# Moving the first table's product, three pairs of stores and a clearing in a kernel of windowed attention and experts

## The chip, the core and the metric

The kernel runs on one core of a Trainium2 chip. A core has five engines with an instruction queue each, and they run side by side: TensorE (PE in the profile, its weight loads PEld) multiplies matrices, VectorE (DVE) and ScalarE (ACT) do elementwise work, GpSimd (POOL) does elementwise work and the indirect transfers, and SyncE (SP) only starts transfers. Each queue is worked off in order; an instruction that waits holds up everything queued behind it on its engine. The metric is device time in microseconds, the median of several runs.

## The reference

Two blocks stand one behind the other. The first is causal attention with a window of 64 positions, over 8 sequences of 576 positions with 8 heads of 64. The second sends each of the 4608 rows of the attention's output to one of 8 experts, by the largest of 8 gate logits, and multiplies the expert's result by the softmax weight of that gate.

```python
scores = scale * np.matmul(q, k.transpose(0, 1, 3, 2))
mask = (rel >= 0) & (rel < window)
scores = np.where(mask, scores, -1000000000.0)
...
x = np.ascontiguousarray(attn_out.transpose(0, 2, 1, 3)).reshape(B * S, H * D)
...
expert_idx = np.argmax(logits, axis=1)
...
h = np.maximum(x_sorted[lo:hi] @ w1[e], 0.0)
y_sorted[lo:hi] = h @ w2[e]
...
return (gate_w[:, None] * y).astype(np.float32)
```

The gate's weight is positive and the hidden layer is a ReLU without bias, so the kernel multiplies the rows by that weight before the experts instead of after them.

## The kernel before

**Attention.** The 8 sequences are taken in four pairs, and each pair's 8 heads in four groups of two heads: 16 units. A unit has 9 blocks of 128 rows, taken three at a time, so there are 48 steps, numbered 0 to 47. `step(s)` is a pipeline written out by hand; on each engine the order of the instructions is the order in which Python emits them:

- the scores of step s+1 (`scored`, TensorE, L697), masked with a running maximum (`masked`, VectorE, L710) and put through the exponential (`softened`, ScalarE, L720). The scores use banks 0 and 1 of PSUM, the memory that TensorE writes; the next step's scores need them back from L710.
- the weighted values of step s-1 (`weighted`, TensorE, L743), into bank 6, which must have been read by the division of the step before (`divided`, VectorE, L753 to L757).
- gate logits of step s-3 (`logit`, L780); the transposes of the exponentials of step s (`flipped`, L728), each half copied out by VectorE or ScalarE (L730); the division; loads for later units; transposes of q and k for step s+3 (`turned`, L656 and L664) and of the finished rows for step s-2 (`x_turned`, L768).
- last, whatever has been put down for this step in the dictionary `todo`.

**Routing.** When the logits of a pair are complete, `after` spreads the pair's routing over the following steps through `todo`. `choose` finds the expert of each row and its rank within the expert (VectorE, L811 to L867, its second half at L847 to L867); `place` writes one-hot rows `lo` with the position within a table column (VectorE, L871, two instructions for each of nine blocks); `weigh` multiplies a block of 128 rows by its gate weight, in place (GpSimd, L882, or ScalarE, L880, for two of the third pair's nine blocks); `store` writes three blocks to `x_dram` (L891, and L898 for the last 64 rows of a sequence).

**First tables.** After the third pair, six steps on, `first_tiles` makes a table `perm_e` of the rows for the first two tiles of expert 0 from the first three pairs: VectorE forms `key` and `hi_e` (L973, L976), TensorE multiplies `lo` by `hi_e` in 54 small products (L983), VectorE turns the result into row numbers (L986). Then `gather_first` clears each of the two halves of `xg` (GpSimd, L293) and fetches rows of `x_dram` into it by indirect transfer (L295). `gather_first` is called a second time behind the loop, for the second tile. The rows are read from `x_dram`, so a fetch waits until the stores have landed.

**Experts.** Behind the loop the first tile is turned (`turn`, L316) and goes through the expert's two products (`hidden`, L354; `output`, L398), each with seven block products instead of eight; the sums of weight blocks that this needs are made by GpSimd (L142, and L1033 for the first weights). The routing of the fourth pair is woven into that tile. Then `expert(e)` runs over the 8 experts with tiles of 256 rows.

**Loads.** `load_qk`, `load_rests` and `load_v` bring q, k and v. `load_rests(bg)` loads the last 64 rows of a pair's sequences: q and k at L624, v at L628. GpSimd copies v into a shifted layout (L636, L638, L642). The queue of SyncE also brings the two halves of the first expert's second weights (L1033, at steps 42 and 45). The end of `after`, for the third pair:

```python
for n in (0, 0, 1, 2, 2):
    do(n, part)
for m in range(NTB):
    do(3 + m // 3, partial(place, bg * NTB + m))
    do((2, 2, 3, 3, 4, 4, 4, 5, 5)[m], partial(weigh, bg, m, nc.scalar if m in (2, 6) else G))
    if m % ST == ST - 1:
        do(3 + m // ST, partial(store, bg, m // ST, G))
do(6, first_tiles)
```

Of the kernel before, what the change touches and what calls it, by code (L numbers as in the profile page):

```python
# [24 lines left out]
def _ins(ap: bass.AP, axis: int, n: int) -> bass.AP:  # L25

    dims = [list(d) for d in ap.ap]
    dims.insert(axis, [0, n])
    return bass.AP(tensor=ap.tensor, offset=ap.offset, ap=dims)


def _inner(ap: bass.AP, n: int) -> bass.AP:
    return _ins(ap, len(ap.ap), n)
# [3 lines left out]
def kernel(  # L37
# [10 lines left out]
    nc = tc.nc  # L48
    P = nc.NUM_PARTITIONS
    B, H, S, D = q.shape  # L50
# [9 lines left out]
    SM = NV * P  # L60
    BG = 2
# [41 lines left out]
    V, G = nc.vector, nc.gpsimd  # L103
# [51 lines left out]
    def sums_w2(e):  # L155
        form(right_sums(G, s2s[e % NW], *w2q(e)))
# [23 lines left out]
    with tc.tile_pool(name="tmp", bufs=1) as tmp:  # L180
# [8 lines left out]
        for i in range(BG):  # L189
# [12 lines left out]
            out=before[:], in_=ones[:], pattern=[[1, P]], compare_op=ALU.is_gt, fill=0.0, base=0,  # L202
# [42 lines left out]
    ST = 3  # L245
# [12 lines left out]
    xg_all = qk_m(0, C, DM)  # L258
    xg = [xg_all[:, c] for c in range(C)]
# [29 lines left out]

    def gather_first(tokens):  # L290

        for c in range(C):
            G.memset(xg[c], 0.0)  # L293

            G.indirect_dma_start(  # L295
                out=xg[c], out_offset=None, in_=x_dram[0 : NT - BG * S, :],
                in_offset=bass.IndirectOffsetOnAxis(ap=tokens[:, c : c + 1], axis=0),
                bounds_check=NT - BG * S - 1, oob_is_err=False,
            )
# [265 lines left out]
    with tc.manual_schedule(), ExitStack() as held, ExitStack() as brief:  # L565
# [51 lines left out]
        def load_rests(bg):  # L617

            at = 6144 + bg % 2 * 2048
            vr = qk_m(at + 1024, BG, H, D)  # L620
            rests[bg] = [qk_m(at, H, D), qk_m(at + 512, H, D), vr]
            for t, src, queue in zip(rests[bg], (q, k), (nc.sync, nc.sync if bg else nc.scalar)):
                for i in range(BG):
                    queue.dma_start(  # L624
                        out=t[i * D : (i + 1) * D], in_=src[bg * BG + i, :, SM:S, :].rearrange("h p d -> p h d")
                    )
            for i in range(BG):
                nc.sync.dma_start(out=vr[D:P, i], in_=v[bg * BG + i, :, SM:S, :].rearrange("h p d -> p h d"))  # L628

        def load_v(u):  # L630
            bg, g = units[u]
# [39 lines left out]
        def blocks_of(t):  # L671

            return [(t // NV, t % NV * 2 + a) if t < BG * NV else (a, NB - 1) for a in range(2)]
# [29 lines left out]
        def masked(s, scs):  # L703

            m0 = (1, 0, 2)[s % NST]
            prs = [att.tile([P, ST, P], F32, name=f"pr{h}") for h in range(2)]
            mx = small.tile([P, 2, ST], F32, name="mx")
            for h in range(2):
                for m in range(ST):
                    V.tensor_tensor_reduce(  # L710
                        out=prs[h][:, m, :], in0=scs[h][:, m, :], in1=mask[:, m0 + m, :], scale=-scale, scalar=-2 * MASKED,
                        op0=ALU.add, op1=ALU.min, accum_out=mx[:, h, m : m + 1],
                    )
            return prs, mx

        def softened(prs, mx):
            for h in range(2):
                for m in range(ST):
                    y = prs[h][:, m, :]
                    nc.scalar.activation(out=y, in_=y, func=AF.Exp, scale=-1.0, bias=mx[:, h, m : m + 1])  # L720
            return prs
# [12 lines left out]
        def weighted(s, pTs):  # L734
            u, c = divmod(s, NST)
            bg, g = units[u]
            va, vb = v_ring[u % NVR]
            px = banks[6 if s < N - 2 else s - N + 2](0, 2, ST, VW)
            for m in range(ST):
                for a, (bp, i) in enumerate(blocks_of(c * ST + m)):  # L740
                    vt = va[:, bp, i // 2] if i % 2 or i == 0 else vb[:, bp, i // 2 - 1]
                    for h in range(2):
                        nc.tensor.matmul(  # L743
                            px[a * D : (a + 1) * D, h, m, :], lhsT=pTs[h][:, m, a * D : (a + 1) * D],
                            rhs=vt[:, h, :], start=True, stop=True, skip_group_check=True,
                        )
            return px
# [25 lines left out]
        def logit(s):  # L773

            u, c = divmod(s, NST)
            bg, g = units[u]
            if g == 0 and c == 0:
                lgs[bg] = banks[7](0, NST, P)[0 : ST * GE]
            for m in range(ST):
                nc.tensor.matmul(  # L780
                    lgs[bg][m * GE : (m + 1) * GE, c, :], lhsT=wg[:, g, :], rhs=xTs[s][:, m * P : (m + 1) * P],
                    start=(g == 0 and c == 0), stop=(g == NG - 1), skip_group_check=True,
                )
            return g == NG - 1
# [113 lines left out]
                    engine.dma_start(out=x_dram[t0 + SM : t0 + S, :], in_=x[i * D : (i + 1) * D, ST - 1, :])  # L898

        gates = {}  # L900
        todo = {}


        def slot_table(hi):
# [42 lines left out]
        def after(s, routing, bg):  # L947

            do = lambda n, op: todo.setdefault(s + n, []).append(op)
            part = lambda: next(routing, None)  # L950
            if bg < last - 1:
                for n in range(5):
                    do(n, part)

                for m in range(NTB):
                    do(5 + m * 2 // 3, partial(place, bg * NTB + m))
                    do(5 + m * 2 // 3, partial(weigh, bg, m, G))
                    if m % ST == ST - 1:
                        do(5 + m * 2 // 3, partial(store, bg, m // ST, G))
                return  # L960
# [4 lines that stand above are left out]
                do(3 + m // 3, partial(place, bg * NTB + m))  # L965
                do((2, 2, 3, 3, 4, 4, 4, 5, 5)[m], partial(weigh, bg, m, nc.scalar if m in (2, 6) else G))
                if m % ST == ST - 1:
                    do(3 + m // ST, partial(store, bg, m // ST, G))
            do(6, first_tiles)

        def first_tiles():

            V.scalar_tensor_tensor(  # L973
                out=key[:], in0=rkhi[:, 0:NJE], scalar=1.0, in1=oh_all[:, 0, 0:NJE], op0=ALU.add, op1=ALU.mult
            )
            V.tensor_tensor(  # L976
                out=hi_e[:], in0=_inner(key[:], NE * C), in1=_ins(hi_id[:, C + 1 : C + 1 + NE * C], 1, NJE),
                op=ALU.is_equal,
            )
            slots = banks[next(tr_ring)](0, NE * C)  # L980
            for j in range(NJE):
                for i in range(2):
                    nc.tensor.matmul(  # L983
                        slots, lhsT=lo[:, i, j], rhs=hi_e[:, j], start=(i + j == 0), stop=(i + j == NJE)
                    )
            V.tensor_scalar(out=perm_e[:], in0=slots, scalar1=-1.0, scalar2=float(NT), op0=ALU.mult, op1=ALU.add)  # L986
            gather_first(perm_e[:, 0:C])

        N = NU * NST
        load_qk(0)  # L990
# [19 lines left out]
        def step(s):  # L1010
            if 0 <= s + 1 < N:
                prs[s + 1] = softened(*masked(s + 1, scored(s + 1)))
            if 0 <= s - 1 < N:
                px = weighted(s - 1, pTs.pop(s - 1))
            ripe = 0 <= s - 3 < N and logit(s - 3)
            if 0 <= s < N:
                pTs[s] = flipped(prs.pop(s))
            if 0 <= s - 1 < N:
                divided(s - 1, px)
            if s >= 0 and s % NST == 0:  # L1020
                u = s // NST
                if u + 3 < NU and (u + 3) % NG == 0:
                    load_rests((u + 3) // NG)
                if u + 2 < NU:
                    load_v(u + 2)
                if u + 3 < NU:
                    load_qk(u + 3)
            if s + 3 < N:
                turned(s + 3)
            if 0 <= s - 2 < N:  # L1030
                x_turned(s - 2)
            for op in todo.pop(s, ()):
                op()  # L1033
            if ripe:
                bg, c = (s - 3) // (NG * NST), (s - 3) % NST
                parts = by_tokens(bg, c)
                next(parts)
                todo.setdefault(s + 1, []).append(partial(next, parts, None))
                if c == NST - 1:
                    after(s + 1, choose(bg), bg)  # L1040
# [4 lines left out]
            todo.setdefault(s, []).append(partial(nc.sync.dma_start, out=w2s[0][:, fs], in_=w2v[0][:, fs]))  # L1045
        for s in range(-3, N):
            step(s)
        assert not todo
        sums_w2(0)


# [45 lines left out]
        table = slot_table(hi)  # L1097
# [134 lines left out]
```

## Time and profile before

| | us |
|---|---|
| median of 3 runs (lowest, highest) | 706.89 (705.32, 711.82) |
| the profiled execution, its own time | 708.33 |
| its span in the profile | 706.5 |
| mean granted clock of TensorE, share of full | 0.989 |
| GpSimd, weighing L882: 25 instructions, each | 1.56 |
| GpSimd, clearing L293: 4 instructions, each | 0.54 |
| GpSimd, fetch of the first tables L295: 4 instructions, each | 1.05 |
| GpSimd, stores L891 and L898: 12 and 6 issues, each | 0.73 and 0.58 |

The profile is one execution, taken by the hardware profiler. In the page a line of a group has the source line, the engine, the operation, output and inputs by their names in the program, the count and the time. A line of the timeline has the start, the time from there to the end of the last merged instruction, the engine, and in brackets how long the engine had been idle and what ended it. A bracket with "issue" means that nothing which the profile shows ended the wait. A wait for several semaphores is put down to the one that came last by the profile; where the engine named had long been done, it was another, often a transfer. The line numbers are those of the kernel before.

### The profile page before, as it was taken

To read this page: it belongs to the slowest core of one execution; us is meant where nothing else is said; L and a number is where in the kernel's file an instruction comes from. 1 tells how busy PE (TensorE), PEld (TensorE's weight loads), DVE (VectorE), ACT (ScalarE), POOL (GpSimd) and SP (SyncE) were. 2 spreads that over 40 slices of the span, in tenths; PEclk is the share of its full clock that TensorE was granted. 3 is DMA by queue.
4 is the path that set the end of the run, shared out by engine and by line. 5 is a ranking of instruction groups with operands and counts; after the bars stand their busy time and mean duration, and the time that the engine had idled before them with its cause. 6 is when DMAs were issued, how large, how long until landed. Compare 5 with 4: busy or idle time off the path is not lost. (4 is left out here: it accounts for less than half of the span.)

```text
span 706.5 us, 18016 instructions
## 1 busy us (share of the span) xinstructions
PE 678.2 (96%) x6894; PEld 594.9 (84%) x6894; DVE 502.8 (71%) x1657; ACT 262.4 (37%) x665; POOL 356.4 (50%) x368
## 2 busy tenths in 40 slices
PE   5999999999889999999999999699999999999996
PEld 4888888888769898897999899599779799789995
DVE  3677998898956868766776586466777676766764
ACT  4888888788745011211111121011121121122211
POOL 4414649487573107856462356437345757254022
PEclk9999999999989999999999999899999999999999
DMA  9987889987433361531701161152127171111022
GB/s 194 221 218 178 185 179 240 217 208 194 164 108 120 107 238 62 216 132 55 266 31 61 59 246 55 64 208 92 62 61 253 61 250 65 63 39 47 16 62 61
DMA packets 137160, 94.64 MB, mean 134 GB/s; under 512 B 116591, under 2 KB 116607, under 8 KB 137024
## 3 DMA queue, kind: packets, MB, share of 16 engines
q1 hardware_dynamic: 114752, 36.19, 21.0%
q0 software_dynamic: 9120, 28.60, 12.4%
q10 hardware_dynamic: 13152, 28.05, 11.2%
q8 instruction: 83, 1.36, 0.8%
q14 instruction: 53, 0.43, 0.2%
HBM read 73.94 MB, written 20.45 MB: 134 GB/s over the span
## 5 line engine op out<-in xcount | busy, mean ns | idle before, releaser
L325 DVE STREAM_TRANSPOSE v_m<-qk_m 32x256 f32<-32x256 f32 x320 | 139.3, 435 | 7.0 <-DMA qk_m<-x_dram,at_g 1.0
L285 POOL DMA_INDIRECT qk_m<-x_dram,at_g x42 | 45.0, 1072 | 169.2 <-DVE v_m L325 160.4
L354 PE MATMUL bank<-qk_m,s 128*128 128x128 f32 x1024 | 123.2, 276 | 0.0
L354 PEld LDWEIGHTS bank<-qk_m,s 128*128 128x128 f32 x1024 | 119.1, 193 | 0.5 <-issue 0.5
L354 PE MATMUL bank<-qk_m,w 128*128 128x128 f32 x768 | 95.8, 278 | 6.2 <-issue 6.2
L720 ACT ACTIVATE pr<-pr,mx 128x128 f32<-128x128 f32 x288 | 89.7, 390 | 31.8 <-DVE mx L710 31.5
L354 PEld LDWEIGHTS bank<-qk_m,w 128*128 128x128 f32 x768 | 91.8, 194 | 9.4 <-issue 9.0
L710 DVE CUSTOM_DVE_ANT_0 pr<-bank,mask 128x128 f32<-128x128 f32 x288 | 64.4, 285 | 24.8 <-PE bank L697 23.6
L305 POOL DMA_INDIRECT out_dram<-v_m,at_s x42 | 42.6, 1013 | 56.6 <-DVE v_m L394 50.5
L394 DVE TENSOR_TENSOR v_m<-bank,v_m 128x256 f32<-128x256 f32 (+1 forms) x95 | 43.7, 479 | 37.8 <-PE bank L398 27.3
L638 POOL COPY v_m<-v_m 64x520 f32<-64x520 f32 x32 | 19.8, 617 | 67.1 <-DMA v_m<-in_v_dram 58.6
L142 POOL TENSOR_TENSOR s<-w 128x1024 f32<-128x1024 f32 x22 | 52.2, 2373 | 0.0
L743 PEld LDWEIGHTS bank<-v_m,pT 128*64 128x64 f32 x1152 | 40.6, 139 | 10.2 <-issue 4.3
L361 ACT COPY qk_m<-bank 128x512 f32<-128x512 f32 x16 | 9.4, 586 | 106.4 <-PE bank L354 80.5
L743 PE MATMUL bank<-v_m,pT 128*64 128x65 f32 x1152 | 47.4, 229 | 1.2 <-DVE xs L757 1.1
L398 PE MATMUL bank<-qkT_m,v_m 128*128 128x256 f32 x216 | 48.3, 379 | 0.0
L697 PE MATMUL bank<-qkT_m 64*64 64x128 f32 x1152 | 45.6, 287 | 0.4 <-DVE mx L710 0.3
L364 DVE TENSOR_TENSOR qk_m<-bank,qk_m 128x512 f32<-128x512 f32 x16 | 11.1, 691 | 48.6 <-PE bank L354 48.6
L398 PEld LDWEIGHTS bank<-qkT_m,v_m 128*128 128x128 f32 x216 | 41.0, 190 | 5.5
L337 ACT COPY qk_m<-v_m 128x512 f32<-128x512 f32 x40 | 22.7, 615 | 61.4 <-DVE v_m L325 61.4
L728 PE MATMUL bank<-ident,pr 128*128 128x128 f32 x288 | 43.3, 288 | 0.0
L664 PE MATMUL bank<-ident,qk_m 128*128 128x128 f32 x256 | 35.8, 286 | 6.8 <-DMA qk_m<-in_q_dram 6.8
(196 smaller groups left out, 1264.4 us busy)
## 6 DMA issues: line engine op xcount, KB each, us to landing
w<-in_moe_w_dram ACTq DMA_DIRECT2D x9, 2048.0 KB, 8.1
qk_m<-in_q_dram SPq DMA_DIRECT2D x72, 128.0 KB, 3.6
qk_m<-in_k_dram SPq DMA_DIRECT2D x66, 128.0 KB, 3.4
v_m<-in_v_dram SPq DMA_DIRECT2D x64, 128.0 KB, 3.2
qk_m<-in_moe_w_dram ACTq DMA_DIRECT2D x3, 2048.0 KB, 10.2
w<-in_moe_w_dram SPq DMA_DIRECT2D x2, 2048.0 KB, 14.2
x_dram<-xs POOLq DMA_DIRECT2D x6, 512.0 KB, 4.8
x_dram<-xs POOLq DMA_DIRECT2D x3, 768.0 KB, 6.2
```

What stands on the lines that cost most here:

```text
L142: op()
L285: G.indirect_dma_start(out=xg[c], out_offset=None, in_=x_dram[:, :], in_offset=bass.IndirectOffsetOnAxis(ap=at_g[:, c : c + 1], axis=0),)
L305: put = G.indirect_dma_start(out=out[:, :], out_offset=bass.IndirectOffsetOnAxis(ap=at_s[:, c : c + 1], axis=0), in_=ys[c], in_offset=None ...
L325: V.transpose(out=xn[b * QD : (b + 1) * QD, :, :, a * QD : (a + 1) * QD].rearrange("p c g i -> p (c g) i"), in_=rows[a * QD : (a + 1) * QD ...
L354: nc.tensor.matmul(acc[:, f, :], lhsT=a[:, g, f * P : (f + 1) * P], rhs=b[:, g, :], start=(first and f == 0 and g == 0), stop=(g == HG - 1 ...
L394: plus = lambda out, a, b: V.tensor_tensor(out=out, in0=a, in1=b, op=ALU.add)
L398: nc.tensor.matmul(acc, lhsT=a[:, f, :], rhs=b[:, f, :], start=(start and f == 0), stop=(stop and f == HF - 1), skip_group_check=True,)
L697: nc.tensor.matmul(out_, lhsT=qT[rows, t, a * WINDOW : (a + 1) * WINDOW], rhs=rhs, start=True, stop=True, skip_group_check=True,)
L710: V.tensor_tensor_reduce(out=prs[h][:, m, :], in0=scs[h][:, m, :], in1=mask[:, m0 + m, :], scale=-scale, scalar=-2 * MASKED, op0=ALU.add, ...
L720: nc.scalar.activation(out=y, in_=y, func=AF.Exp, scale=-1.0, bias=mx[:, h, m : m + 1])
L728: nc.tensor.transpose(out=tr[:, m, :], in_=prs[h][:, m, :], identity=ident[:])
L743: nc.tensor.matmul(px[a * D : (a + 1) * D, h, m, :], lhsT=pTs[h][:, m, a * D : (a + 1) * D], rhs=vt[:, h, :], start=True, stop=True, skip_ ...
```

## The change

Four edits:

- `first_tiles` becomes a generator in two parts. The first part, `key` and `hi_e`, stays where it was, in `todo` six steps on (step 45). The second part, the 54 products, `perm_e` and the fetch, goes into a new dictionary `between`, for the step after that (step 46), where `step` runs it behind the scores and the weighted values and ahead of the gate logits.
- The stores of the third pair go from GpSimd's queue to SyncE's.
- `gather_first` clears both halves of `xg` with one instruction ahead of both fetches.
- The v rows of the first pair's last 64 positions are loaded from GpSimd's queue instead of SyncE's.

On TensorE the 54 products move behind 24 score products and 24 value products; on VectorE the instruction that makes `perm_e` moves behind six of the mask (L710); on SyncE six stores stand between the two halves of the weights of L1033. No product, copy or byte is added or removed.

```diff
     def gather_first(tokens):
 
+        G.memset(xg_all, 0.0)
         for c in range(C):
-            G.memset(xg[c], 0.0)
-
             G.indirect_dma_start(
...
             for i in range(BG):
-                nc.sync.dma_start(out=vr[D:P, i], in_=v[bg * BG + i, :, SM:S, :].rearrange("h p d -> p h d"))
+                (nc.sync if bg else G).dma_start(out=vr[D:P, i], in_=v[bg * BG + i, :, SM:S, :].rearrange("h p d -> p h d"))
...
-        todo = {}
+        todo, between = {}, {}
...
                 if m % ST == ST - 1:
-                    do(3 + m // ST, partial(store, bg, m // ST, G))
-            do(6, first_tiles)
+                    do(3 + m // ST, partial(store, bg, m // ST, nc.sync))
+            table = first_tiles()
+            do(6, partial(next, table))
+            between.setdefault(s + 7, []).append(partial(next, table))
...
                 op=ALU.is_equal,
             )
+            yield
             slots = banks[next(tr_ring)](0, NE * C)
...
             V.tensor_scalar(out=perm_e[:], in0=slots, scalar1=-1.0, scalar2=float(NT), op0=ALU.mult, op1=ALU.add)
             gather_first(perm_e[:, 0:C])
+            yield
...
             if 0 <= s - 1 < N:
                 px = weighted(s - 1, pTs.pop(s - 1))
+            for op in between.pop(s, ()):
+                op()
             ripe = 0 <= s - 3 < N and logit(s - 3)
...
-        assert not todo
+        assert not todo and not between
```

## The prediction

> **What bounds the kernel now.** I read the busy shares first, then whom TensorE waited for, then stretches around the place that the change touches, and last the instructions there in order of time. Times in parentheses are starts in us of the one profiled execution. The shares, from the page:
>
> ```profile
> PE 678.2 (96%) x6894; PEld 594.9 (84%) x6894; DVE 502.8 (71%) x1657; ACT 262.4 (37%) x665; POOL 356.4 (50%) x368
> ```
>
> TensorE is busy for 678.2 of 706.5 us, so only 28.3 us of idling can be won at all, plus time at a low clock. The list of waits shows 6.8 us of it on the first q loads and 2.7 us on `hi_e` (L976), the operand of the first table's product. The stretches around that wait:
>
> ```profile
> 174.00:184.00 10.00, 8.34 (x143) 6.68 (x141) 8.55 (x50) 7.01 (x22) 3.90 (x4) 1.00 0.30 108
> 184.00:196.00 12.00, 11.41 (x202) 9.16 (x201) 11.85 (x54) 9.38 (x26) 8.95 (x8) 1.00 0.62 218
> 196.00:199.00 3.00, 0.29 (x11) 0.25 (x10) 2.60 (x19) 2.60 (x8) 2.70 (x4) 1.00 0.22 53
> 199.00:206.00 7.00, 7.00 (x114) 5.82 (x110) 2.65 (x17) 2.34 (x7) 3.45 (x5) 0.51 0.42 133
> 206.00:210.00 4.00, 4.00 (x68) 3.33 (x68) 1.92 (x7) 1.34 (x3) 3.89 (x3) 1.00 0.24 70
> ```
>
> Columns: stretch, length, busy time (and count) of TensorE, its weight loads, VectorE, ScalarE, GpSimd, then the granted clock. VectorE is full from 184 to 196 and TensorE is not; TensorE stands still from 196 to 199; then it runs at a clock of 0.51 for seven microseconds. In order of time:
>
> ```profile
> 195.55 0.49 PE L768 MATMUL bank<-ident,xs 128*128 128x128 f32 x3
> 196.86 0.55 DVE L730 COPY pT<-bank 128x384 f32<-128x384 f32 x1
> 198.43 0.27 DVE L976 TENSOR_TENSOR hi_e<-key,hi_id 128x108 bf16<-128x108 bf16 x1
> 198.75 1.56 PE L983 MATMUL bank<-hi_e,lo 128*128 128x4 bf16 x54 [2.71 <-DVE hi_e L976]
> 200.24 1.56 PE L697 MATMUL bank<-qkT_m 64*64 64x128 f32 x24
> 201.73 1.62 PE L743 MATMUL bank<-v_m,pT 128*64 128x65 f32 x24
> 203.04 1.13 POOL L295 DMA_INDIRECT qk_m<-x_dram,perm_e  x1 [3.28 <-DVE mx L710]
> 203.85 1.54 PE L728 MATMUL bank<-ident,pr 128*128 128x128 f32 x6
> 205.97 0.97 PE L743 MATMUL bank<-v_m,pT 128*64 128x65 f32 x24
> ```
>
> The product L983 is queued ahead of scores (L697) and weighted values (L743) that do not need it. The gather's wait is put down to VectorE's L710, but `perm_e` was done at 200.58; what ended it were the stores into `x_dram`, the last issued at 198.66 (their row: 2.3 to 4.8 us to landing). After 206, TensorE's largest waits carry no releaser but "issue" (6.2 us, at branches) and the rest sum to 3 us: what it gains before L316 (209.56) reaches the end one for one.
>
> **What the Trainium skill says here.** (1) TensorE: Matmul & The Clock Gate, "What's actually happening": the clock halves after an idle window of about 3.4 us, free-running, and comes back after a busy one. The trace agrees: 2.71 us of idling was followed by 0.51; 1.42 us at 182.3 was not. (2) SBUF — State Buffer, "Who interferes with whom": VectorE and GpSimd share a port pair as a lock; copies, casts, tensor_scalar and two-SBUF-input operations can be blocked. It agrees: six `lo` instructions (L871) take 1.33 us (184.49 to 185.82) with GpSimd idle, 2.40 (188.45 to 190.84) and 2.14 (193.46 to 195.60) beside its weighing. The lock is not held throughout, though: L814 took its usual 0.28 beside a weighing (123.55). (3) DMA: Bandwidth & Descriptors, "Two DMAs through the same engine are not ordered": a read of what a DMA wrote must wait for its completion, as the gather does. (4) Same page, "Latency and other measured facts": first byte about 0.6 us from SyncE's path, 1 us from GpSimd's.
>
> **The change, part by part.**
>
> *The product behind scores and values.* At stake: idling from 196.04 (195.55+0.49) to 198.75, 2.71 us, and the cold stretch. From 198.75 to 205.97, 7.22 us, TensorE does L983, L697, L743, L780, L728, L768. Warm, start to start, the same groups took 0.82, 0.90, 0.35, 0.71 and 0.42 (188.28 to 191.70); L983 took 1.49 cold, halved 0.75 (an estimate). Sum 3.95, so coldness costs 3.27. In the new order the scores wait for their bank, which L710 frees at 196.94: start 197.1, idle 1.06, end 197.9. The values wait for L757 (198.30) and ScalarE's copy of `pT` (198.45): start 198.6, idle 0.6 to 0.7. `hi_e` is ready at 198.70, so L983 runs at 199.5 without waiting. Then L780, L728, L768 to 201.7. VectorE does L710 from 198.7 to 200.0, `perm_e` to 200.5, L730 to 201.6, L753 to L757 to 202.5; the next values start at 202.65, idle about 0.85. Before: 205.97. **Gain 3.3 us**: 5.98 at stake less about 2.6 of new waits. If the clock fell nevertheless, 3.3 come back.
>
> *`perm_e` on VectorE* (0.16 us) now stands behind six L710; its only reader is the gather. Cost 0.
>
> *Stores of the third pair on SyncE.* GpSimd loses six issues, 0.82+1.32+0.60+0.75+0.56 = 4.05 us, and this:
>
> ```profile
> 186.97 0.82 POOL L891 DMA_DIRECT2D x_dram<-xs  x1 [8.07 <-issue]
> ```
>
> It stood 8.07 us for ScalarE's share of the weighing (L880, 185.70 to 186.43) with five weighings queued behind. Freed, its seven (1.56 each) run from 175.79 to 186.7, not to 197.0. SyncE issues in order behind L880's second part (189.77 to 190.52): six stores at 0.33 to 0.58, last by about 193; with 4.8 us they land by 198, not 203. Behind them on SyncE stands only `w2`'s second half: from 188.06 to about 193.5, landing at most 6.5 later, by 200; its reader, the second L142, comes at about 205. Cost 0. The gather then waits for `perm_e`: 200.7 instead of 203.04.
>
> *One clearing.* Two memsets of 0.54 become one of about 1.07, done in GpSimd's idle time. The second gather follows at 1.3 us (as at 244.08 and 245.39) instead of 1.94: 202.0, landing 3.4 later at 205.4. L316 comes at 209.56-3.3 = 206.2: not waiting, 0.8 in hand. GpSimd's L142 (9.4 us) and second gathers shift too; they keep about 3.5 us ahead of L316 at 225.68. Value 0, but without these edits the gather's old landing, 208.4, would eat 2.2 of the 3.3.
>
> *First v rests by GpSimd.* SyncE's queue moves up 1.36 us (6.75 to 8.11). TensorE's only waits for loads are ahead of that, so 0. GpSimd issues two transfers behind L992 (9.36); the trace has no such row, nearest is L991, 0.98, so to 11.3, landing (3.7 to 4.3) by 15.6. L636 moves from 11.38 to there, but the next copy waits for v until 17.62 anyway. Bounds: -0.3 (less crowding ahead of the 0.60 us wait) to +1.0 (copies later than L743 at 19.17, slack 0.37). I take 0.
>
> *The shared port, not in the diff.* Weighing moves from 187.8-197.0 to 178.9-186.7. Relief for L871: 1.07+0.81 = 1.9. In return the routing chain L847 to L867 (179.18 to 181.95, 2.77 us, GpSimd idle then) is stretched: by L871's ratio 2.27/1.33, +2.0. VectorE runs without a gap from there to `hi_e`, so these nearly cancel; I take 0. Bounds: -1.9 (no stretch) to +2.9 (blocked until 186.7, +4.8, less 1.9).
>
> **Sum:** -3.3. The profiled execution: 706.5 span, 708.33 in all, to 705.0. It lay 1.44 above the median of 706.89 (705.32 to 711.82); against the median, **703.6**. A measurement here tells about 1% (7 us) from no change, so this lies within.
>
> **Rivals.**
> 1. *The cold stretch moves forward.* The stretched chain delays L710 and L730; TensorE's gap at 182.3 grows from 1.42 to 3.4 us, the size of a window. Then about 3.3 us are lost there: -3.3+3.3, **706.9**. For it: VectorE is the bound there. Against: the stretch is only inferred. Chance 0.27.
> 2. *Slower: the port lock at the routing chain.* Each of its ten or so instructions loses to a weighing, up to the end of weighing at 186.7: +4.8-1.9, and the gap surely cools the clock, +3.3: -3.3+2.9+3.3 = +2.9, **709.8**. It decides from a stretch of 2.0 us with a cold clock, 5.2 without. For it: L820 took 1.16 instead of 0.23 beside a GpSimd sum (79.95). Against: L814. Chance 0.14.
> 3. *The idling stays where it was*, another operand (bank, `pT`) taking `hi_e`'s place and cooling the clock again: only 2.71-2.6, **706.8**. Chance 0.10.
> 4. *The gain is larger*, over 7 us, which only a second stall that I do not see could give: about 699. Chance 0.04.
>
> **Numbers.** My forecast 0.45, own range 701.2 to 705.5 (no stretch at all: -5.2; some new waits longer: -1.4). The range 700.8 to 708.4 takes in cases 1 and 3 with the 1.0 of the v rests, and leaves out 2 and 4. Over 1% faster 0.10 (case 4 and a low draw), within 0.82, slower 0.08 (a larger form of case 2).
>
> **What would show it.** Right: L983 behind L743 with no wait on `hi_e`; clock 1.00 from 196 on; GpSimd's weighings in one block ending near 187; the gather waiting for `perm_e` only, L316 not waiting for it. Wrong: L847 to L867 longer than 2.8 us, a gap over 2.5 us before L768 near 183, a clock below 0.9 anywhere between 180 and 206, or L743 later than 19.2 at the start.

## The result, and the profile after

The changed kernel takes 705.33 us (median of 20 runs, 703.58 to 708.72), the kernel before 708.15 us (705.32 to 712.52) in as many. The ratio is 0.9956, 95% interval 0.9942 to 0.9969: **faster by 0.44%**, 3.1 us by the ratio. The profiled execution spans 703.6 us, against 706.5 before. In the changed kernel the line numbers stand a little differently: scores L696, mask L709, values L742, `pT` L729, `x_turned` L767, routing L846 to L866, `lo` L870, weighing L881, product L985, fetch L294, turn L315, hidden layer L353.

First the stretches that were shown of before (start and end, length, busy time and count of TensorE, its weight loads, VectorE, ScalarE, GpSimd, then the granted clock):

```profile
174.00:184.00 10.00, 7.71 (x138) 6.18 (x136) 8.64 (x46) 5.58 (x18) 9.34 (x8) 1.00 0.29 107
184.00:196.00 12.00, 11.49 (x194) 9.38 (x194) 10.73 (x55) 10.60 (x30) 3.25 (x3) 0.86 0.63 219
196.00:199.00 3.00, 2.52 (x44) 2.09 (x43) 2.90 (x20) 2.60 (x8) 0.00 (x0) 1.00 0.81 270
199.00:206.00 7.00, 7.00 (x145) 5.78 (x143) 4.14 (x22) 3.58 (x10) 3.38 (x3) 1.00 0.22 54
```

The stand from 196 to 199 us (0.29 busy before, 2.52 now) is gone, and so is the clock of 0.51 behind it. But a clock of 0.86 has appeared from 184 to 196. TensorE's timeline of the changed kernel shows both ends of this:

```profile
178.97 0.97 PE L742 MATMUL bank<-v_m,pT 128*64 128x65 f32 x24
...
184.51 0.62 PE L767 MATMUL bank<-ident,xs 128*128 128x128 f32 x3 [2.55 <-DVE pT L729]
185.06 1.56 PE L696 MATMUL bank<-qkT_m 64*64 64x128 f32 x24
186.54 1.62 PE L742 MATMUL bank<-v_m,pT 128*64 128x65 f32 x24
...
198.69 1.02 PE L742 MATMUL bank<-v_m,pT 128*64 128x65 f32 x24 [0.48 <-DVE xs L756]
199.65 1.51 PE L985 MATMUL bank<-hi_e,lo 128*128 128x4 bf16 x54
...
202.64 1.22 PE L742 MATMUL bank<-v_m,pT 128*64 128x65 f32 x24
...
206.47 1.46 PE L315 MATMUL bank<-ident,qk_m 128*128 128x128 f32 x8
```

The product stands behind the values and waits for nothing. The same place near 184 us in the kernel before:

```profile
183.74 0.55 PE L768 MATMUL bank<-ident,xs 128*128 128x128 f32 x3 [1.42 <-DVE pT L730]
184.21 0.89 PE L697 MATMUL bank<-qkT_m 64*64 64x128 f32 x24
185.03 0.97 PE L743 MATMUL bank<-v_m,pT 128*64 128x65 f32 x24
```

The gap ahead of L767 is 2.55 us, where it was 1.42, and the scores and values behind it take the cold 1.56 and 1.62 us instead of 0.89 and 0.97. What made the gap longer is VectorE's routing chain (L846 to L866), beside GpSimd's weighing. Two timelines of the changed kernel, and between them the first and the last instruction of the chain in the kernel before, where no weighing stands beside them:

```profile
178.82 0.55 DVE L846 TENSOR_TENSOR_SCAN r_inc<-keep,r_ranks 128x72 f32<-128x72 f32 x1
...
180.21 0.63 DVE L856 TENSOR_TENSOR r_rank<-r_rank,r_ranks 128x72 f32<-128x72 f32 x1
...
181.69 0.62 DVE L864 CAST rkhi<-r_half 128x9 f32<-128x9 int32 x1
...
182.56 0.64 DVE L866 CAST low<-r_half 128x9 f32<-128x9 int32 x1
```

```profile
179.18 0.30 DVE L847 TENSOR_TENSOR_SCAN r_inc<-keep,r_ranks 128x72 f32<-128x72 f32 x1
...
181.78 0.17 DVE L867 CAST low<-r_half 128x9 f32<-128x9 int32 x1
```

```profile
175.43 10.82 POOL L881 TENSOR_SCALAR xs<-xs,gate 128x512 f32<-128x512 f32 x7 [0.62 <-DVE gate L841]
...
202.29 1.16 POOL L294 DMA_INDIRECT qk_m<-x_dram,perm_e  x1 [15.04 <-DVE perm_e L988]
203.76 1.02 POOL L294 DMA_INDIRECT qk_m<-x_dram,perm_e  x1 [0.31 <-issue]
```

Four instructions that take 0.17 to 0.30 us without company take 0.55 to 0.64, about one for each weighing that passes (10.82/7 = 1.55 us). From its start to the first mask behind it the chain takes 3.8 us instead of 2.7. The weighing is one block, and what releases the fetch is `perm_e`.

### The profile page after: what moved, and what is told of

Its sections match the earlier page's. It is cut to its first block, busy times and chain, and to the rows that moved or that the text cites. A ratio compares the mean times of both kernels' runs of the same rounds, so it can differ in the third digit from the quotient of the medians.

```text
span 703.6 us, 18017 instructions
## 1 busy us (share of the span) xinstructions
PE 674.5 (96%) x6894; PEld 591.9 (84%) x6894; DVE 502.6 (71%) x1657; ACT 262.5 (37%) x665; POOL 354.7 (50%) x362
## 5 line engine op out<-in xcount | busy, mean ns | idle before, releaser
L353 PE MATMUL bank<-qk_m,s 128*128 128x128 f32 x1024 | 122.4, 275 | 0.0
L353 PEld LDWEIGHTS bank<-qk_m,s 128*128 128x128 f32 x1024 | 118.3, 192 | 0.0
L353 PE MATMUL bank<-qk_m,w 128*128 128x128 f32 x768 | 95.8, 278 | 6.6 <-issue 6.6
L353 PEld LDWEIGHTS bank<-qk_m,w 128*128 128x128 f32 x768 | 92.0, 194 | 10.1 <-issue 9.7
L709 DVE CUSTOM_DVE_ANT_0 pr<-bank,mask 128x128 f32<-128x128 f32 x288 | 64.5, 288 | 20.3 <-PE bank L696 18.0
L742 PEld LDWEIGHTS bank<-v_m,pT 128*64 128x64 f32 x1152 | 41.3, 139 | 11.9 <-issue 4.2
L742 PE MATMUL bank<-v_m,pT 128*64 128x65 f32 x1152 | 48.5, 229 | 2.5 <-DVE xs L756 1.1
L696 PE MATMUL bank<-qkT_m 64*64 64x128 f32 x1152 | 44.3, 282 | 0.8 <-DVE mx L709 0.8
```

Source lines behind the costliest of these rows:

```text
L353: nc.tensor.matmul(acc[:, f, :], lhsT=a[:, g, f * P : (f + 1) * P], rhs=b[:, g, :], start=(first and f == 0 and g == 0), stop=(g == HG - 1 ...
L696: nc.tensor.matmul(out_, lhsT=qT[rows, t, a * WINDOW : (a + 1) * WINDOW], rhs=rhs, start=True, stop=True, skip_group_check=True,)
L709: V.tensor_tensor_reduce(out=prs[h][:, m, :], in0=scs[h][:, m, :], in1=mask[:, m0 + m, :], scale=-scale, scalar=-2 * MASKED, op0=ALU.add, ...
L742: nc.tensor.matmul(px[a * D : (a + 1) * D, h, m, :], lhsT=pTs[h][:, m, a * D : (a + 1) * D], rhs=vt[:, h, :], start=True, stop=True, skip_ ...
```

## The experiments

The table puts all of them side by side; the ratio is to the kernel before in runs on the same chip. "Start" is when the values of step 42 begin, the last ones ahead of the gap near 184 us; "section" runs from there to the first hidden-layer product; "gap" is TensorE's idle time ahead of L767 near 184, "clock" the mean granted one from 184 to 196 us; "tail" runs from the end of the last store's issue to the end of the span. All but the ratios come from one profiled execution each.

| kernel | ratio (95%) | start | section | gap | clock | tail |
|---|---|---|---|---|---|---|
| before | | 179.3 | 32.0 | 1.42 | 1.00 | 4.2 |
| before_again | 1.0010 (0.9985 to 1.0034) | 181.6 | 32.0 | 1.41 | 1.00 | 4.3 |
| product_only | 1.0047 (1.0032 to 1.0062) | 182.5 | 31.2 | 1.42 | 1.00 | 4.4 |
| stores_only | 1.0074 (1.0041 to 1.0107) | 178.8 | 31.8 | 2.55 | 0.86 | 9.3 |
| stores_only_spare | 0.9988 (0.9962 to 1.0014) | 182.9 | 30.5 | 2.54 | 0.86 | 4.9 |
| v_only | 0.9971 (0.9954 to 0.9989) | 177.7 | 31.2 | 1.42 | 1.00 | 4.4 |
| product_v | 0.9998 (0.9976 to 1.0020) | 179.5 | 31.6 | 1.42 | 1.00 | 4.4 |
| v_by_sync | 1.0056 (1.0036 to 1.0077) | 180.2 | 31.0 | 2.55 | 0.72 | 9.3 |
| v_by_sync_spare | 0.9987 (0.9968 to 1.0007) | 181.5 | 30.4 | 2.54 | 0.86 | 4.5 |
| the changed kernel | 0.9956 (0.9942 to 0.9969) | 179.0 | 29.6 | 2.55 | 0.86 | 4.5 |
| two_clearings | 0.9952 (0.9935 to 0.9970) | 179.8 | 30.5 | 2.54 | 0.86 | 4.7 |
| gate_late | 0.9949 (0.9932 to 0.9966) | 177.6 | 30.2 | 2.01 | 0.90 | 4.3 |
| weigh_scalar | 0.9923 (0.9895 to 0.9951) | 179.7 | 28.2 | 1.66 | 1.00 | 4.9 |
| no_gpsimd_weighing | 0.9896 (0.9863 to 0.9928) | 177.6 | 27.1 | 1.42 | 1.00 | 4.3 |

**One edit alone, one edit undone.** Product_only is the kernel before with nothing but the generator and `between`; stores_only has nothing but the stores' new queue; two_clearings is the changed kernel with the old clearing:

```diff
-                    do(3 + m // ST, partial(store, bg, m // ST, G))
+                    do(3 + m // ST, partial(store, bg, m // ST, nc.sync))
```

```diff
-        G.memset(xg_all, 0.0)
         for c in range(C):
+            G.memset(xg[c], 0.0)
```

> The kernel before with one edit: the 54 products stand behind the next scores and values. Theory A (the product's place is the source of the gain, and the fetch then limits it): no wait for hi_e, clock near 1.00 after 196 us, but GpSimd still ends its weighing near 197 and the stores land near 203, so the fetches start near 203 and 205 as before and L316 waits for the second until about 208; ratio to before 0.997 to 0.999. Rival B (the stores are the source): ratio 1.000. If the fetch does not limit: 0.994.

> The kernel before with one edit: SyncE stores the third pair. Theory A: GpSimd's weighing runs in one block to about 187, VectorE's routing chain is stretched by about 1.1 us beside it and TensorE goes cold for one window there; TensorE still waits for hi_e near 199, but less (about 1.9 instead of 2.7 us, since it comes later), so whether it goes cold a second time is open: ratio 0.997 without, 1.001 with it. Rival B: 0.996, all of the gain.

> The changed kernel with a clearing ahead of each fetch again. Theory A: the second fetch follows the first at 1.9 instead of 1.45 us, and L316 waits about 0.5 us longer for it: ratio to before 0.9960 to 0.9967. Rival (the fetch is hidden): 0.9956.

And the changed kernel with the first v rests back on SyncE:

```diff
-                (nc.sync if bg else G).dma_start(out=vr[D:P, i], in_=v[bg * BG + i, :, SM:S, :].rearrange("h p d -> p h d"))
+                nc.sync.dma_start(out=vr[D:P, i], in_=v[bg * BG + i, :, SM:S, :].rearrange("h p d -> p h d"))
```

> The changed kernel with the first v rests back on SyncE. Theory A: TensorE's only wait for loads at the start is for what is loaded ahead of them; the lead of 1.3 us at 22 us was down to 0.4 by 34 us; ratio to before 0.9956 to 0.9965. Rival C (a third or more of the gain is the earlier start): 0.997 or more.

For only one of the four did a forecast hold as it was meant: the rival's for two_clearings (0.9952, no difference). Each large edit alone made the kernel slower, and undoing the small one cost 1%, more than the whole change had brought. For stores_only and v_by_sync the table says where: not in the attention part, but in a tail of 9.3 us.

**The tail.** In v_by_sync the last store is issued at 701.49 + 1.00, as early as in the kernel before (702.3), and the span ends at 711.8. The lines of the program's end show GpSimd's last drains (operation, count; shortest, median and longest in ns; first and last start), first v_by_sync, then the changed kernel:

```profile
L1232 POOLq DRAIN  x3: 46/109/9148, 701.8 to 711.5; - x3
```

```profile
L1232 POOLq DRAIN  x3: 46/109/4245, 698.4 to 703.4; - x3
```

No engine works in those nine microseconds, and the longest drain is 4.9 us longer. Another trace shows itself a few instructions earlier. Among the late transfers of GpSimd in the kernel before, one waits 1.90 us for nothing that the profile names; in the changed kernel another one waits 1.53:

```profile
678.13 1.02 POOL L305 DMA_INDIRECT out_dram<-v_m,at_s  x1 [1.90 <-issue]
```

```profile
694.48 0.99 POOL L285 DMA_INDIRECT qk_m<-x_dram,at_g  x1 [1.53 <-issue]
```

The kernel before issues 108 transfers from GpSimd, and the pause lies ahead of the fifth from the end; the changed kernel issues 104 (six stores less, two loads more), and it lies ahead of the third from the end. Stores_only and v_by_sync issue 102; there all late transfers follow with the usual 0.3 to 0.4 us, and the long drain comes instead. So the theory was that the pause comes after a certain amount of GpSimd's transfers, hidden where it falls ahead of a transfer and seen where it falls on the end of the program. If so, two more transfers of any kind must take it out of the tail:

```diff
                 nc.sync.dma_start(out=vr[D:P, i], in_=v[bg * BG + i, :, SM:S, :].rearrange("h p d -> p h d"))
+                if bg == 0:
+                    G.dma_start(out=vr[0:D, i], in_=v[bg * BG + i, :, SM:S, :].rearrange("h p d -> p h d"))
```

> The changed kernel with the first rows of v again by SyncE, and two further loads of the same rows by GpSimd at the place in its queue where the v loads stood; they go into a part of the buffer that nobody reads. So only who brings the v rests differs from the changed kernel, and the number of GpSimd's transfers is the changed kernel's (104, not 102). Tail theory: v_by_sync lost about 5 us after its last store was issued (GpSimd's last drain 9.1 us instead of 4.2, span end 9.3 us after that issue ended instead of 4.5), because of how many transfers GpSimd's queue had handled. Then this one has a last drain of 4 to 5 us and a ratio near 1.0056 - 0.0069 = 0.999, down to 0.9955 if the start costs nothing. Start theory: v by SyncE is what costs, through copies and first values; then the ratio stays at 1.0056 within 0.002 and the drain says nothing of it.

> The kernel before with the third pair's stores on SyncE alone, and the same two further loads on GpSimd (104 transfers instead of 102). Tail theory: last drain of 4 to 5 us instead of 9.1; ratio 1.0074 - 0.0069 = 1.0005, within 0.998 to 1.002, which is what the stores alone are worth while the product still stands ahead of the scores. Theory that the stores hurt in the attention part: ratio stays at 1.005 or more and the drain at 9.

With 104 transfers both tails are short again (4.5 and 4.9 us), the pause is back ahead of the last gather (1.53 us in both), and the ratios fell by 0.0069 and 0.0086: **5 to 6 us hung on two transfers that nobody reads**. That what GpSimd has issued decides the tail is shown. What is counted is open: the pause stands behind 103 transfers in the kernel before and behind 101 in the changed kernel, so it isn't their number alone, and with 110 transfers (v_only and product_v) no such pause shows at all. The Trainium skill (DMA: Bandwidth & Descriptors, "SWDGE vs HWDGE vs iDMA") says that GpSimd itself writes the descriptors of its transfers into rings, and that only one queue of this kind is allocated. No run here shows the rings or what the pause is.

So stores_only and v_by_sync say nothing of the attention part by their times, and the spare versions take their place. **The stores alone are worth 0.9988**, not distinguishable from nothing.

**The first v rests.** The changed kernel and v_by_sync_spare differ only in who brings the v rests (v_by_sync_spare's two idle loads stand in their place on GpSimd, and both have the pause of 1.53 us at the same transfer), and the ratios are 0.9956 and 0.9987: 2.2 us, where the prediction had 0. To see it without any other edit, and the spread of doing nothing beside it:

```diff
-                nc.sync.dma_start(out=vr[D:P, i], in_=v[bg * BG + i, :, SM:S, :].rearrange("h p d -> p h d"))
+                (nc.sync if bg else G).dma_start(out=vr[D:P, i], in_=v[bg * BG + i, :, SM:S, :].rearrange("h p d -> p h d"))
```

> The kernel before with the first v rests loaded by GpSimd and nothing else changed (110 transfers of GpSimd, last drain about 4 us, so that the tail is that of the kernel before). Start theory, from the changed kernel against v_by_sync_spare (0.9956 against 0.9987): SyncE's queue runs 1.4 us earlier and the first values no longer wait for v (1.7 to 1.9 us in the executions of product_only and v_by_sync_spare, none or 0.7 with GpSimd): 1.5 to 3 us faster, ratio 0.996 to 0.998; step 42 by 179.0. The prediction's step: worth 0, ratio 0.9985 to 1.0015.

> The kernel before, once more, as a measure of what no change at all gives. Product_only has the same instructions on every engine up to 190 us, and yet its profiled execution reached the values of step 42 at 182.5 us where the one of the kernel before had 179.3. Theory that the start differs from execution to execution: ratio within 0.9985 to 1.0015, and the values of step 42 anywhere from 178 to 183 us. Theory that the start of a kernel is fixed and product_only's is slow for a reason of its own: 179.3 within 0.3 us.

V_only has 0.9971, 2.1 us: the same again, and outside the interval of the unchanged kernel run once more (the two intervals just overlap). Before_again has the same instructions as the kernel before, and yet its profiled execution reaches step 42 at 181.6 us instead of 179.3. The seven executions with v on SyncE lie between 178.8 and 182.9 us (mean 181.0), the seven with v on GpSimd between 177.6 and 179.8 (mean 178.7). TensorE's waits in the first 60 us (what waited, for what, total, times, longest), before_again and then v_only:

```profile
PE bank L664 <- DMA qk_m<-in_q_dram: 4.7, 1, 4.7
PE bank L743 <- ACT pr L720: 1.5, 1, 1.5
PE bank L743 <- DVE mx L710: 1.2, 1, 1.2
PE bank L743 <- POOL v_m L642: 0.8, 1, 0.8
```

```profile
PE bank L664 <- DMA qk_m<-in_q_dram: 6.2, 2, 5.8
PE bank L743 <- POOL v_m L642: 0.7, 1, 0.7
```

In before_again the first weighted values (L743) wait 2.7 us more. In product_only and v_by_sync_spare 1.9 and 1.7 us of it is put down to the loads of v themselves. Those are queued on SyncE behind the v rests: they start at 13.75 us in the kernel before and at 11.83 in v_only. GpSimd's first copy of v, which waits for them, moves up with them (the kernel before, then v_only):

```profile
17.62 0.62 POOL L638 COPY v_m<-v_m 64x520 f32<-64x520 f32 x1 [5.95 <-DMA v_m<-in_v_dram]
```

```profile
16.38 0.62 POOL L638 COPY v_m<-v_m 64x520 f32<-64x520 f32 x1 [2.74 <-DMA v_m<-in_v_dram]
```

The waits alone would mislead, since the first q come at another time in each execution. The end of the first weighted values is a better mark: 20.14 us in the kernel before, 20.27 in before_again, 18.35 in v_only; over the seven executions with v on SyncE 18.8 to 20.9 (mean 19.9), over the seven with v on GpSimd 17.9 to 18.8 (mean 18.4). So about 1.6 of the 2.3 us between the two means at step 42 are there from the first values on.

**The product without the stores.** Product_only had a late start (182.5 us) by the same kind of waits. With the v rests on GpSimd the product's own effect can be read:

```diff
+                (nc.sync if bg else G).dma_start(out=vr[D:P, i], in_=v[bg * BG + i, :, SM:S, :].rearrange("h p d -> p h d"))
...
+            for op in between.pop(s, ()):
+                op()
```

> The kernel before with the product behind scores and values and the first v rests by GpSimd; the third pair's stores stay on GpSimd, ahead of the fetch. If product_only's 1.0047 came from its start, this one starts like the changed kernel and has the product's gain of 2 to 3 us less the wait of L316 for the late fetch (1.2 us in product_only): ratio 0.996 to 0.999. If the product's place costs time by itself: 1.0015 or more.

0.9998 fits neither. Against v_only (0.9971) the product's move cost 1.9 us instead of bringing 2 to 3, though the two intervals overlap at their ends. The timeline of product_v shows why:

```profile
205.19 1.21 PE L743 MATMUL bank<-v_m,pT 128*64 128x65 f32 x24
207.39 0.65 PE L316 MATMUL bank<-ident,qk_m 128*128 128x128 f32 x4 [0.99 <-DMA qk_m<-x_dram,perm_e]
209.12 0.69 PE L316 MATMUL bank<-ident,qk_m 128*128 128x128 f32 x4 [1.08 <-DMA qk_m<-x_dram,perm_e]
211.02 2.91 PE L354 MATMUL bank<-qk_m,w 128*128 128x128 f32 x16
```

From the values of step 42 (179.45) to the last values (205.19) it takes 25.74 us, v_only 28.27 (177.69 to 205.96): 2.5 us gained. Then L316 waits 2.07 us for the fetch, which the stores on GpSimd's queue hold back until 203.78, and the first hidden products run cold, 2.91 us instead of 1.95. From the values of step 42 to the next hidden products it takes 35.23 us, in v_only 33.86: the gain is given back, and 1.4 us with it. **Without the stores' move the product's move is worth nothing, or less.** What it adds to the stores' move isn't shown: with stores and clearing 0.9987 (v_by_sync_spare), the stores alone 0.9988, and neither is clear of 1. Product_only's 1.0047, a loss of 3.3 us, is more than the 1.9 here, though no instruction ahead of 190 us differs from the kernel before; what remains, some 1.4 us, stays open.

**What the stores' move costs.** In the table the gap tells two groups apart. Where the stores stand on GpSimd's queue and split the weighing in three, it is 1.41 or 1.42 us and the clock stays at 1.00 (five rows). Where the weighing runs in one block beside the routing chain, it is 2.54 or 2.55, and the clock falls (six rows). Three versions of the changed kernel test it: the gate, which the weighings read, behind the chain; no weighing on GpSimd at all, which leaves the weighting of these rows out of the computation; and three weighings on GpSimd, six on ScalarE.

```diff
-            gate_of()
+            if bg != last - 1:
+                gate_of()
...
             V.tensor_copy(out=low[:, js], in_=half[:])
+            if bg == last - 1:
+                gate_of()
```

> The changed kernel with the gate's arithmetic of the third pair done behind the routing chain instead of ahead of it, so that GpSimd's weighings, which read the gate, start only after the chain. Shared port theory: the chain is back to about 2.7 us (3.8 in the changed kernel), TensorE's gap at 184 shrinks from 2.55 to about 1.5 us, and the clock stays at 1.00 over 184 to 196 us (0.86). VectorE bounds that stretch, so of the 3.4 us cold window only a part is TensorE's loss: 0.3 to 1.5 us faster than the changed kernel, ratio 0.9935 to 0.9952. Rival: the weighings then fall on the lo instructions and hi_e, as before the change, and take back what is gained: ratio 0.9955 to 0.998 though the clock is 1.00.

```diff
-                do((2, 2, 3, 3, 4, 4, 4, 5, 5)[m], partial(weigh, bg, m, nc.scalar if m in (2, 6) else G))
+                if m in (2, 6):
+                    do((2, 2, 3, 3, 4, 4, 4, 5, 5)[m], partial(weigh, bg, m, nc.scalar))
```

> The changed kernel without GpSimd's seven weighings of the third pair: these rows are stored unweighted, so that part of the computation is left out. Nothing of GpSimd then stands beside VectorE from 176 to 186 us. Shared port theory: the routing chain takes 2.7 us, no gap over 2 us at 184, clock 1.00 from 180 to 206: 1 to 2 us faster than the changed kernel, ratio 0.9928 to 0.9942, which is the most that a better place for the weighings can give. Rival: the gap at 184 comes from VectorE's own work (masks, copies, chain), the clock falls there as well: ratio 0.995 to 0.997.

```diff
-                do((2, 2, 3, 3, 4, 4, 4, 5, 5)[m], partial(weigh, bg, m, nc.scalar if m in (2, 6) else G))
+                do((2, 2, 2, 2, 3, 3, 4, 4, 5)[m], partial(weigh, bg, m, nc.scalar if m > 2 else G))
```

> The changed kernel with the third pair's weighing shared out anew: GpSimd three (m = 0, 1, 2), done by about 180.2 us, before most of the routing chain; ScalarE six at 0.73 us each instead of two, the first of them early, where ScalarE is 56 to 70% busy. Shared port theory: without any weighing on GpSimd the kernel was at 0.9896 (0.9863 to 0.9928), so half to two thirds of that is to be had: ratio 0.992 to 0.9945, chain 2.8 to 3.1 us, clock 1.00 over 184 to 196. Rival: ScalarE is nearly full from 184 on (10.6 of 12 us), its copies for TensorE come later by 0.7 us a step and take the gain back: ratio 0.9955 to 0.999.

Without the weighings the gap is back to 1.42, the clock stays at 1.00, and the section is 2.5 us shorter than in the changed kernel. So GpSimd's weighing costs the changed kernel 2.5 us in the profile and 4.2 by the ratios (0.9956 and 0.9896), more than the 1 to 2 that were expected. The chain beside it is where the 1.1 us of the gap come from; that all of the rest comes from VectorE isn't shown, since this version also has less to wait for. Gate_late's ratio lies in the range that was forecast, but not for the reason that was given: its chain is short again (2.7 us), and yet the gap is 2.01 and the clock falls all the same. The edit itself lengthened the gap: the gate's three instructions now stand between the chain and the masks and hold them from 180.18 to 180.83 us. The clock is halved from 183.1 us for 3.4 us, as long as in the changed kernel (the 0.90 of the table sees only a part of it), and again behind 200 us, and weighing now stands beside `lo`, where six instructions take 1.7 us instead of 1.3. Against the changed kernel 0.9949 is no difference. Weigh_scalar did in the profile what was expected; its windows:

```profile
184.00:196.00 12.00, 10.73 (x195) 8.70 (x196) 11.35 (x65) 12.00 (x33) 0.00 (x0) 1.00 0.17 62
196.00:199.00 3.00, 2.93 (x66) 2.45 (x65) 2.82 (x17) 2.83 (x10) 0.00 (x0) 1.00 0.67 216
199.00:206.00 7.00, 7.00 (x133) 5.77 (x130) 3.69 (x17) 2.99 (x9) 4.12 (x3) 1.00 0.85 247
```

The clock is 1.00 throughout and the section 1.4 us shorter than the changed kernel's, though ScalarE is full (12.00 of 12.00). Its ratio, 0.9923, is the lowest of the complete kernels, but the interval (0.9895 to 0.9951) overlaps the changed kernel's: faster than before is shown, faster than the changed kernel is not.

## Why the prediction was right, and where it was not

The forecast, 3.3 us faster, lies 0.2 us from the 3.1 that the ratio gives. That agreement is in good part luck. The sum held; two of its terms did not, and they missed in opposite directions: by the ratios 2.1 to 2.2 of the 3.1 us come from the edit that was put at nothing. Of the signs that the prediction had named for being wrong three came: the routing chain at 3.8 us (limit 2.8), the gap near 184 at 2.55 (limit 2.5) and a clock of 0.86 between 184 and 196 (limit 0.9). Of the signs for being right all came but one: L315 does wait for the fetch, 0.4 us.

- **The product behind scores and values: gain 3.3.** The mechanism is right to the step: no wait for `hi_e`, clock 1.00 from 196 on, and the next values at 202.64 us, forecast 202.65. But that time agrees because errors met. From the last L767 ahead of the product (195.55 before, 196.70 now) to the next values it takes 5.94 us instead of 10.42, a gain of 4.5; 1.5 us were lost ahead of it, at the first gap and in the cold stretch behind it, and the start of this execution was 0.35 us earlier. The two profiled executions alone would have seemed to confirm the term; the runs of v_only and v_by_sync_spare don't. L985 was estimated at 0.75 us warm, half its cold time; the next group, L779, starts 1.44 us after it, about as long as it took cold (1.49).
- **Stores on SyncE: cost 0.** Right for what was named: weighing ends at 186.2 (forecast 186.7), the fetch waits for `perm_e` only, w2's second half is issued at 192.96 (forecast 193.5). That without this edit the fetch would eat 2.2 us was right too: 2.07 in product_v.
- **The shared port: net 0.** This step failed. The stretch of the chain was 1.1 us, not 2.0, and the relief for `lo` came in the later steps (0.22 us each instead of about 0.38), but the sum left out what the gap does to the clock. A gap of 2.55 us sufficed for the cold stretch that rival 1 had tied to a gap of 3.4 us. So forecast and rival 1 both came in part. Product, stores and clearing together are worth 0.9987 (v_by_sync_spare), 0.9 us with an interval from a gain of 2.3 to a loss of 0.5, instead of 3.3.
- **First v rests: 0, bounds -0.3 to +1.0.** This step failed as well: -2.1 us, twice measured. The argument was that TensorE's only waits for loads lie ahead of these transfers. That was so in the one profiled execution (0.5 us of waits behind them); before_again, the same kernel, waits 4.5 us there. What the step overlooked is that v itself stands behind these transfers in SyncE's queue: the copy that it took to wait "for v until 17.62 anyway" came at 16.38 us in v_only. The first-byte times that the prediction quoted, 0.6 and 1 us, show in no run; from issue to landing the v rests took a median of 4.1 us by either queue in v_only.
- **One clearing: 0.** Right (0.9956 and 0.9952). The second fetch followed at 1.47 us. The 0.8 us in hand at L315 were not there: its eight products take 1.46 us instead of 1.09 and wait for the second fetch.
- **The tail** was in no step. Removing six transfers from GpSimd and adding two kept the pause out of it; with the v edit left out, the same change measured 1.0056, slower (v_by_sync). That it went well is luck.

## What to carry to other kernels

A slack that one profiled execution shows isn't the slack of the kernel: where loads start the work, look at several executions, or at what stands behind the load in its queue. When a queue is freed, ask what its work will now run beside: here the weighing moved onto a chain that TensorE waits for. When a change has several edits, measure each alone and all but each: here the smallest edit brought most. And compare the time from the last issued store to the end of the span before explaining a difference of a few microseconds by the part that was edited.

## What the runs showed that was not expected

- The end of a program can cost 5 us more or less with the transfers that GpSimd has issued: 102 gave tails of 9.3 us, 104, 108 and 110 gave 4.2 to 4.9.
- How long an idle stretch must be to cool the clock is not one number. The same wait of 1.89 us for `hi_e` was followed by 0.76 from 199 to 206 us in stores_only and by no fall in stores_only_spare; gaps of 1.42 and 1.66 never cooled it, 2.01 to 2.71 always did; and from 199 to 206 us two_clearings, v_by_sync_spare and gate_late show 0.76, 0.85 and 0.76 behind waits of 0.48 us. Nor is the length of the cold stretch: the same wait of 2.7 us was followed by about 6.8 us at half clock in the kernel before and in before_again and by 3.4 in v_only. The Trainium skill (TensorE: Matmul & The Clock Gate, "What's actually happening") has a free-running window of 3.4 us, so that it matters where in the window the gap falls; that agrees (cold stretches of 3.4 and 6.8 us are one and two such windows), but a gap far shorter than the window, 2.01 us, was enough here.
- The 54 products of bf16 with four columns take 27 ns each at full clock (1.44 us in all) and hardly more at half (1.49).
- GpSimd's weighing doesn't hold VectorE off for its whole 1.55 us. In the routing chain it costs about 0.4 us about once per weighing. That isn't a fixed price: the second six `lo` instructions of the kernel before lost 1.1 us within 2.4, beside hardly more than one and a half weighings.
